# Odd heads across the partition halves by copies instead of products, with w_out's pieces first and a new list of steps

## The chip, the cores and the metric

The kernel runs on one core of one Trainium2 chip, in one launch. The metric is the device time of one execution in microseconds; the median of several runs is compared. "The profile" is one profiled execution: what each engine did and when, with the transfers (DMA).

## The reference, cut to what matters

A delta-rule attention (4 batches, 8 heads, 768 tokens, 48 features per head) is followed by a feed-forward part of three products. All is float32.

```python
k_n = k / (np.linalg.norm(k, axis=-1, keepdims=True) + 1e-06)
for t in range(S):
    kt, vt, bt = (k_n[:, :, t], v[:, :, t], beta[:, :, t, None])
    y[:, :, t] = np.einsum('bhd,bhde->bhe', q[:, :, t], state)
    v_old = np.einsum('bhde,bhd->bhe', state, kt)
    state = state + bt[:, :, :, None] * np.einsum('bhd,bhe->bhde', kt, vt - v_old)
# x: the outputs y, one row of 384 features for each of 3072 tokens
a = x @ w1                # 384 x 1024
b = x @ w2                # 384 x 1024
h = a * b @ w3            # 1024 x 1024
return h @ w_out          # 1024 x 384
```

## The kernel before, in words

**Attention.** The 768 tokens are cut into 12 chunks of 64. A chunk holds all four batches and eight heads at once: two batches lie on partitions 0 to 63, the other two on 64 to 127 (`half(z)`), and odd heads lie crossed, on the other half. The recurrence becomes, for each chunk, the inverse of a triangular 64x64 matrix for each batch and head. Two chunks share an inverse: their 32x32 diagonal blocks lie one on each partition, and VectorE eliminates them in 31 steps of two instructions (`inverse`, step names V0 to V5, lines 492 and 497 for the first two inverses, 503 and 508 for the rest). The off-diagonal 32x32 block is made with two rounds of small products (`corner`, steps e0 to e11, line 584). For the first four chunks (`TURNED`) the blocks come and go by copies, and the second round of products needs the second diagonal block of the odd heads on the other partition half: `X22`. Before the change, two products with the identity (line 598) write it into PSUM, and ScalarE copies it out (line 617).

**Norms.** `squares` (steps g0 to g5) has GpSimd square the keys of two chunks and VectorE sum them; `norms` (N0 to N5) takes the inverse norms by three Newton steps on VectorE. Both end in `across`, which moves the odd heads' numbers to the other partition half: before the change two products with the identity into a PSUM bank (line 278), then a copy of the even heads (line 283) and one out of PSUM (line 284). The banks are handed out in turn; `skip` lets one turn pass.

**Weights.** w3 and w_out are folded into one matrix of 1024 x 384, `w34` (`fold`, steps f0 to f7, line 864), since h is only used for h @ w_out. A fold takes eight matmuls, in two halves of four, and needs all of w_out and one row block of w3, transposed (`transpose_w3`, steps t0 to t15, line 855, ScalarE's copy at line 858). The weights arrive in pieces (`piece`, steps P0 to P35): P0 to P7 are w_out (128 x 384), P8 to P23 are w3 (128 x 512; P8 and P9 serve fold f0, P10 and P11 fold f1 and so on), P24 to P35 are w1 and w2. They come in 64-bit words, so each piece is a transfer on SyncE's queue into one of five `raw` buffers (line 804), two ScalarE instructions (812, 813), two on VectorE (815, 816) and an addition on GpSimd (820), which frees the buffer.

**Feed-forward.** For the first pair of chunks, `ab` multiplies x by w1 and w2 directly (line 884); the later pairs are done by `eleven` (line 1003) with sums of weights and tokens made on GpSimd, so that seven block products stand for eight. `o` multiplies by `w34` (line 1113), also with seven products, and `store` writes the result.

**Order.** Each part is a generator; a step runs it to its next `yield`. `ORDER` lists all steps by name, and every engine then works in the order in which the steps put instructions on its queue (`in_text_order`). A waiting instruction holds up all that is behind it on its engine; the transfers on SyncE's queue also go in that order. Each part has a letter of its own: k, q, v and p for loads (p in the layout for VectorE's transposes), K and Q for TensorE's transposes of the first two chunks, d for VectorE's, s for scores, u for the move of blocks to the inverse, c for the chain of states, y for the outputs, a, h, i, j for `eleven`, S and G for sums, o and x for the result.

Of the kernel before, what the change touches and what calls it, by code (L numbers as in the profile page):

```python
# [36 lines left out]


ORDER = """
V0 P0 k0 beta P18 P13 P0 P18 P0 P0 P18 P18 g0 P11 beta P13 K0 K0 P11 P10 beta P13 P13 q0 P10 g0  # L40
g0 K0 K0 K0 P11 Q0 P11 P10 P3 P3 k1 g0 g0 P12 P8 P9 P3 Q0 Q0 Q0 g0 g0 g0 g0 Q0 s0 g0 N0 P3 P10 k2
q1 P8 P8 P9 s0 P12 s0 P2 P8 s0 s0 s0 u0 K1 K1 p2 P5 K1 K1 K1 P12 g1 t3 P2 P2 P12 Q1 Q1 P2 u0 P1
P9 P9 Q1 Q1 Q1 u0 t2 s0 t2 d2 d2 P5 s1 s1 P4 s1 P5 s1 s1 s1 g1 P1 P1 g1 g1 P6 t3 u1 u1 N0 N0 t0
P5 u1 t10 V0 V0 P7 P14 V0 V0 V0 t1 P4 P4 t5 t0 P1 f1 P6 V0 V0 P4 P6 P6 V0 V0 V0 t10 t1 t5 P7 f0
P7 P7 f0 P16 V0 V0 V0 P14 P14 V0 V0 P16 P16 t4 t4 f1 f2 P19 P19 s0 f1 f2 P14 s1 f0 V0 P19 t6 V0
V0 P19 V0 P17 k3 p2 v1 t11 P17 P17 P17 P15 t6 f2 f5 t11 P16 V0 V0 g1 V0 V0 V0 V0 V1 P15 P15 P15
t9 t9 f5 f5 V0 v0 V0 t8 t8 V0 f3 t7 P20 P20 P20 f4 P22 V0 t7 f3 V0 V0 P23 P20 P21 P24 V0 P22 V0
V0 P22 V0 d2 f3 P22 f4 t14 g1 g1 g1 g1 t12 e0 e0 e0 e0 f4 g1 d2 p3 e0 s2 N1 s2 s2 P26 t14 f7 e1
P21 e1 e0 e0 P26 t12 e1 P21 P21 P24 s2 n0 e0 n0 f6 p3 d3 d3 c0 P23 e1 P30 p4 s2 s2 P23 P23 d3 u2
c0 e1 d3 e1 y0 s3 P26 P26 t13 y0 P24 n1 t15 s3 s3 P30 u2 s3 P24 s3 s3 c0 c0 t15 P30 f7 c1 t13 n1  # L50
u3 u3 u2 u3 V1 c1 P25 P31 P25 e1 P25 P31 P30 P31 P31 V1 V1 P32 V1 V1 V1 V1 V1 V1 f7 e1 f6 P27 P25
P32 c1 c1 y0 b0 f6 s1 y1 V1 b2 V1 V1 P27 y1 b3 b3 v2 P32 P28 b2 P32 V1 V1 V1 V1 b1 b0 V1 N1 N1
P29 P27 n2 P28 P28 P28 b0 b0 V1 y1 V1 V1 b1 b1 b1 c1 a03 P35 a01 P27 P29 P29 P29 V1 V1 V1 a01 a03
a02 V1 V1 V1 P33 d4 P34 V1 V1 V1 b7 V1 V2 a02 d4 a05 a05 b7 a00 k4 g2 a01 a01 a04 a04 V1 V1 V1
a06 a00 V1 V1 P33 a06 a02 a02 b3 b3 g2 a00 a00 c1 g2 g2 a07 P35 P34 e2 e2 e2 a07 b5 b5 k5 e2 b2
e2 P34 P33 p4 d4 d4 c2 v3 g2 g2 n2 c2 P33 P35 P35 g2 b4 e2 e2 n3 n3 e2 b6 c2 c2 e3 b6 b2 a03 y2
c2 b4 e3 P34 g2 g2 a04 e3 a03 p5 d5 d5 p5 y2 b4 c2 e3 e3 e3 k6 g2 s4 N2 s4 b7 b7 b4 a04 s4 s4 s4
e3 s4 b6 T u4 T T s4 e3 d5 d5 N2 b6 s5 s5 s5 s5 s5 s5 s5 s5 a06 a06 N2 T a07 a05 a07 u5 c3 c3 b5
b5 V2 g3 a05 g3 p6 v5 V2 V2 c3 c3 V2 oD0 y3 v4 g3 V2 y3 y3 V2 V2 V2 V2 oA0 V2 V2 V2 V2 d6 V2 S0
S0 S0 S0 W d6 S0 S0 S0 g3 S0 S0 c3 V2 xA0 oB0 xB0 V2 V2 V2 oA0 k7 V2 V2 S0 S0 S0 V2 S0 S0 S0 V2  # L60
oB0 xB0 V2 xA0 xA0 G1 oC0 a10 a10 a10 S0 xC0 xC0 V2 a10 V2 V2 oC0 xC0 a10 xD0 a10 V2 h10 s4 V2
i10 a12 a12 h10 h10 V2 j10 V2 V2 V2 V2 V2 h10 W W xC0 i10 g3 c3 V2 g3 V2 j12 n4 a12 i12 xD0 a12
a12 p6 d6 h10 d6 c4 g3 g3 a12 n5 n4 V2 g3 g3 i10 e4 c4 h12 e4 a11 p7 e4 W h12 h12 a11 e4 e4 i12
e5 i12 e4 N3 h12 s6 s6 s6 s6 j11 c4 c4 a11 y4 y4 a11 h12 h11 c4 d7 d7 e5 e5 p7 c4 a11 i11 c5 n5
a11 h11 c5 e5 e5 e5 h11 a13 k8 g4 d7 d7 s7 h11 s7 a13 s7 s7 s7 s7 s7 i11 i11 a13 h11 a13 u7 s6 s6
c5 c5 h13 u6 s6 a13 a13 h13 i13 i13 h13 j13 h13 h13 S1 s6 V3 V3 V3 g4 p8 V3 y5 y5 V3 V3 V3 V3 V3
i13 S1 V3 V3 v6 y5 oC1 d8 V3 oA1 S1 S1 g4 V3 V3 V3 V3 d8 n6 oD1 V3 V3 xA1 S1 oA1 v7 n7 c5 V3 V3
V3 S1 V3 xA1 oB1 xB1 g4 xA1 a20 S1 a20 V3 V3 V3 oB1 j20 xB1 xC1 k9 p8 V3 S1 xD1 V3 V3 V3 V3 G2
oC1 a20 a20 h20 xC1 xC1 a20 V3 V3 a20 h20 i20 V3 V3 V3 a22 a22 i20 V3 V3 xD1 xC1 h20 h20 h20 j22
g4 c5 g4 g4 a22 a22 d8 h22 i20 a22 V3 e6 i22 g4 d8 p9 a22 h22 h22 N3 e6 N3 i22 e6 e6 n6 h22 s7 c6  # L70
c6 a21 h22 i22 a21 a21 e6 g4 g4 N4 i21 e6 c6 s8 c6 h21 a21 s8 v8 s8 s8 n8 V4 a21 a21 h21 y6 d9 d9
s8 i21 j21 i21 y6 h21 a23 e7 s8 e7 c6 c6 s8 e7 e7 p9 i23 h21 h21 s8 e7 n7 d9 d9 a23 a23 a23 s9
k10 g5 s9 e7 s9 s9 s9 s9 a23 u8 c7 h23 s9 u9 c7 c7 a23 h23 h23 h23 V4 c7 i23 i23 S2 j23 S2 y7 h23
V4 g5 V4 V4 V4 V4 oA2 S2 S2 oD2 S2 S2 p10 V4 V4 V4 V4 V4 V4 V4 v9 V4 y7 y7 G3 c7 k11 V4 oB2 V4 V4
xA2 oA2 S2 xB2 oB2 V4 V4 V4 d10 d10 V4 V4 xB2 s9 xD2 V4 oC2 a30 a30 xC2 xC2 xD2 V4 V4 a30 V4 V4
a30 xA2 S2 oC2 xC2 p10 xA2 V4 V4 j30 h30 V4 V4 a30 c7 a30 h30 i30 i30 i30 xC2 a32 a32 V4 V4 V4 V4
h30 d10 V4 V4 j32 h30 h30 n8 e8 a32 d10 h32 a32 a32 a32 c8 c8 N4 i32 h32 i32 e8 h32 e8 h32 e8 N4
g5 g5 g5 g5 g5 a31 a31 p11 g5 a31 e8 a31 e9 g5 j31 e8 g5 N5 c8 c8 i31 h32 y8 c8 d11 a31 y8 d11
p11 h31 e9 a31 s10 c8 i32 h31 i31 i31 e9 s10 a33 a33 s10 n9 e9 h31 s10 s10 s10 s10 e9 e9 a33 a33
j33 c9 d11 d11 s11 h31 s11 s11 u10 a33 S3 V5 h31 h33 v10 n9 c9 c9 s11 s11 a33 h33 s11 u11 c9 i33  # L80
i33 i33 S3 V5 h33 h33 h33 s11 s11 y9 V5 y9 oA3 oD3 S3 S3 xA3 n10 V5 V5 V5 V5 S3 y9 V5 V5 V5 V5 V5
oB3 oC3 xB3 S3 V5 G4 V5 V5 V5 V5 oB3 xB3 oA3 S3 xD3 xC3 xC3 V5 V5 xD3 a40 a40 a40 S3 oC3 s10 n10
xA3 xA3 a40 a40 V5 V5 xC3 i40 a40 V5 V5 V5 V5 h40 h40 c9 i40 i40 V5 a42 a42 V5 V5 V5 h40 h40 a42
j40 a42 h42 h40 V5 V5 V5 V5 a42 a42 V5 i42 a41 h42 V5 V5 v11 h42 h42 i42 i42 V5 j42 a41 a41 n11
h42 i41 a41 a41 n11 h41 c9 a41 h41 j41 V5 e10 e10 e10 e10 c10 c10 i41 h41 h41 h41 a43 e10 e11 i41
N5 a43 N5 a43 a43 h43 e10 e11 e11 e11 c10 c10 j43 a43 a43 h43 c10 c10 e11 e11 i43 h43 i43 i43 h43
h43 c11 c11 y10 y10 c11 oD4 oA4 S4 xC3 S4 S4 xA4 S4 S4 c11 y11 y11 y11 oB4 oA4 xA4 oC4 S4 S4 S4
xA4 xB4 oB4 G5 xB4 xC4 a50 a50 a50 a50 oC4 a50 xC4 xC4 h50 xD4 a50 h50 i50 i50 i50 h50 h50 xD4
j50 a52 a52 a52 a52 i52 h50 a52 h52 a52 h52 i52 j52 h52 h52 h52 a51 a51 a51 a51 h51 a51 a51 i51
i52 S5 a53 a53 h51 h51 h51 j51 i51 i51 a53 h53 h51 a53 a53 j53 a53 h53 h53 i53 h53 h53 xC4 i53  # L90
i53 o5 o5 x5 o5 x5 S5 S5 S5 S5 x5 o5 o5 S5 S5 S5 o5 x5 x5 x5 x5 x5 x5 x5 o5 x5 x5 x5 x5
"""


# [1 line left out]
def kernel(  # L96
# [14 lines left out]
    P = 128  # L111
# [21 lines left out]
    def half(z):  # L133
        return slice(C * z, C * z + C)
# [17 lines left out]
    def skip(tag):  # L152
        turns[tag] = turns.get(tag, -1) + 1

    def two_banks():
        return in_turn(psW, [P, 2, 512], "w", 2, "ps_w")

    def bank(shape):
        return in_turn(psF, shape, "f", 4, "ps_f")
# [107 lines left out]

    def across(src, dst, j):

        n = src.shape[1]  # L270
        ps = bank([P, CW]) if j < 3 else two_banks()[:, 0]
        ps = ps[:, 0 : n * NR * NP].rearrange("p (c r a) -> p c r a", c=n, r=NR)
        odd, even = (
            x.rearrange("p c r (a e) -> p e (c r) a", e=2) for x in (src, dst)
        )
        psv = ps.rearrange("p c r a -> p (c r) a")
        for z in range(2):
            pe.matmul(
                psv[half(1 - z)], lhsT=ident[half(z), half(z)], rhs=odd[half(z), 1],
                start=True, stop=True,  # L280
            )
        yield
        dve.tensor_copy(out=even[:, 0], in_=odd[:, 0])
        dve.tensor_copy(out=even[:, 1], in_=psv)
        yield

    def squares(j):
# [265 lines left out]
    def corner(m):  # L553
# [38 lines left out]

        if turned:
            L = late_pad
            ps2 = two_banks()
            other22 = ps2[:, 1, N // 2 : N].rearrange("p (g t) -> p g t", t=BS)
            for z in range(2):
                pe.matmul(
                    other22[half(1 - z)], lhsT=ident[half(z), half(z)],
                    rhs=TT[half(z), :, :, BS:C].rearrange("p r (a e) t -> p e (r a) t", e=2)[:, 1],  # L600
                    start=True, stop=True,
                )
            ps = products(
                lambda n, z: (U[rows(z), C * n : C * n + C], z ^ n % 2),
                lambda n, z: T11[rows(z), BS * n : BS * n + BS],
                half, ps2,
            )
        else:
            L = T11
            ps = products(  # L610
                lambda n, z: (U[rows(z), C * n + BS : C * n + C + 1], z ^ n % 2),
                lambda n, z: T11[rows(z), BS * n : BS * n + BS],
            )
        yield
        if turned:
            X22 = in_turn(work, [P, 256], "tb", 2, "tb")[:].rearrange("p (g t) -> p g t", t=BS)
            act.copy(out=X22, in_=other22)
        for z in range(2):
            x = quarter(2 * z + turned)
            act.copy(  # L620
# [682 lines left out]
```

## Time and profile before

| | us |
|---|---|
| median of 3 runs (lowest, highest) | 558.83 (557.52, 559.52) |
| the profiled execution | 559.79 |
| its span, first to last instruction | 558.0 |
| TensorE busy | 527.2 (94%) |
| VectorE busy | 392.0 (70%) |
| GpSimd busy | 253.2 (45%) |
| ScalarE busy | 181.8 (33%) |

In the page's slices a digit is the busy share in tenths of one fortieth of the span (13.95 us). PE is TensorE's matmul, PEld its weight load, DVE is VectorE, ACT ScalarE, POOL GpSimd, SP SyncE; a "q" behind the name is the queue that issues transfers. An instruction's row gives start, duration, engine, line, operation, output and inputs with partitions x elements, and in brackets the idle time before it and what ended it. A TensorE matmul in float32 leaves two records. Matmuls overlap, so that the cost of a group is read from its start to the next group's start.

### The profile page before, as it was taken

To read this page: it belongs to the slowest core of one execution; us is meant where nothing else is said; L and a number is where in the kernel's file an instruction comes from. 1 tells how busy PE (TensorE), PEld (TensorE's weight loads), DVE (VectorE), ACT (ScalarE), POOL (GpSimd) and SP (SyncE) were. 2 spreads that over 40 slices of the span, in tenths; PEclk is the share of its full clock that TensorE was granted. 3 is DMA by queue.
4 is the path that set the end of the run, shared out by engine and by line. 5 is a ranking of instruction groups with operands and counts; after the bars stand their busy time and mean duration, and the time that the engine had idled before them with its cause. 6 is when DMAs were issued, how large, how long until landed. Compare 5 with 4: busy or idle time off the path is not lost.

```text
span 558.0 us, 20019 instructions
## 1 busy us (share of the span) xinstructions
PE 527.2 (94%) x8604; PEld 452.7 (81%) x8604; DVE 392.0 (70%) x874; ACT 181.8 (33%) x361; POOL 253.2 (45%) x270
## 2 busy tenths in 40 slices
PE   3569999999999999999999999999999999999997
PEld 2456667678888998889988889988899888998897
DVE  4989989899875998568886569976658855123422
ACT  4686558954541212332012430122220112300000
POOL 8576443643549793154631448121384022441141
PEclk9977999999999999999999999999999999999999
DMA  8976975668545635346534662453322031010001
GB/s 249 222 199 186 196 177 95 163 135 159 79 65 100 111 78 105 54 74 128 104 79 76 93 117 44 86 104 52 60 64 71 15 73 27 6 54 15 2 0 58
DMA packets 197689, 52.67 MB, mean 94 GB/s; under 512 B 185344, under 2 KB 191488, under 8 KB 197600
## 3 DMA queue, kind: packets, MB, share of 16 engines
q1 hardware_dynamic: 193408, 50.59, 44.0%
q10 hardware_dynamic: 4192, 0.79, 1.0%
q8 instruction: 68, 1.11, 0.8%
q14 instruction: 21, 0.17, 0.1%
HBM read 41.25 MB, written 8.91 MB: 90 GB/s over the span
## 4 chain that ended last, share of the span: by engine, by line
PE 85%; DMA 7%; ACT 3%; SPq 3%; issue 1%; DVE 1%; POOL 0%; ACTq 0%; DVEq 0%
PE ps_f L1003 35%; PE ps_f L1113 19%; PE ps_f L884 7%; PE ps_w L663 6%; PE ps_f L864 5%; PE ps_w L759 4%; PE ps_w L584 2%; DMA raw<-in_moe_w_dram 2%; DMA raw<-in_moe_w_out_dram 2%; SPq L251 2%; PE ps_w L391 1%; PE ps_w L397 1%; DMA X<-in_q_dram 1%; PE ps_w L1113 1%; DMA ktok<-in_k_dram 1%
## 5 line engine op out<-in xcount | busy, mean ns | idle before, releaser
L1011 DVE TENSOR_TENSOR ab<-ab,ps_f 128x512 f32<-128x512 f32 x80 | 54.3, 684 | 45.1 <-PE ps_f L1003 43.8
L1050 POOL TENSOR_TENSOR ab<-ab,late 128x512 f32<-128x512 f32 x19 | 24.2, 1276 | 121.7 <-DVE ab L1011 115.6
L1003 PE MATMUL ps_f<-xT,w1s 128*128 128x256 f32 x320 | 78.6, 382 | 0.0
L1084 POOL TENSOR_TENSOR ab<-ab 128x512 f32<-128x512 f32 (+1 forms) x56 | 61.3, 1119 | 32.9 <-PE ps_f L1113 23.2
L1003 PEld LDWEIGHTS ps_f<-xT,w1s 128*128 128x128 f32 x320 | 59.9, 190 | 8.0 <-issue 0.2
L1113 PE MATMUL ps_f<-w,ab 128*128 128x192 f32 x376 | 65.0, 327 | 0.0
L1113 PEld LDWEIGHTS ps_f<-w,ab 128*128 128x128 f32 x376 | 61.5, 190 | 0.8 <-issue 0.2
L1019 ACT COPY ab<-ps_f 128x512 f32<-128x512 f32 x20 | 11.7, 587 | 121.6 <-PE ps_f L1003 121.6
L503 DVE TENSOR_TENSOR tb<-ps_w,Ub 128x31 f32<-128x31 f32 (+15 forms) x124 | 42.0, 338 | 8.7 <-ACT ps_w L483 4.7
L1113 PE MATMUL ps_f<-room,ab 128*128 128x192 f32 x272 | 47.6, 329 | 0.0
L864 PE MATMUL ps_f<-w2s,w3T 128*128 128x384 f32 x128 | 45.4, 506 | 1.4 <-ACT w3T L858 0.8
L508 DVE TENSOR_TENSOR ps_w<-ps_w,tb 128x31 f32<-128x31 f32 (+15 forms) x124 | 43.3, 349 | 4.2
L780 ACT COPY xT<-ps_w 48x256 f32<-48x256 f32 x96 | 30.5, 366 | 47.9 <-PE ps_w L759 44.8
L1113 PEld LDWEIGHTS ps_f<-room,ab 128*128 128x128 f32 x272 | 44.3, 190 | 0.7 <-issue 0.3
L1003 PE MATMUL ps_f<-xT,room 128*128 128x256 f32 x160 | 41.1, 384 | 0.0
L293 POOL TENSOR_TENSOR sq<-ktok 128x384 f32<-128x384 f32 x24 | 21.0, 884 | 43.4 <-DMA ktok<-in_k_dram 26.3
L1003 PE MATMUL ps_f<-xT,w2s 128*128 128x256 f32 x160 | 40.0, 382 | 0.0
L864 PEld LDWEIGHTS ps_f<-w2s,w3T 128*128 128x128 f32 x128 | 24.4, 197 | 17.5 <-issue 2.5
L1003 PE MATMUL ps_f<-x_room,w2s 128*128 128x256 f32 x160 | 38.5, 384 | 0.0
L417 POOL TENSOR_TENSOR PT<-PT,smask 128x512 f32<-128x512 f32 x20 | 25.5, 1280 | 27.7 <-ACT PT L415 18.9
L820 POOL TENSOR_TENSOR w<-w,raw 128x512 uint32<-128x512 uint32 x16 | 20.7, 1296 | 30.4 <-DVE w L816 15.6
L1003 PEld LDWEIGHTS ps_f<-x_room,w2s 128*128 128x128 f32 x160 | 29.7, 190 | 4.8 <-DVE late L1011 0.7
(158 smaller groups left out, 1042.5 us busy)
## 6 DMA issues: line engine op xcount, KB each, us to landing
raw<-in_moe_w_dram SPq DMA_DIRECT2D x16, 512.0 KB, 5.4
vtok<-in_v_dram SPq DMA_DIRECT2D x24, 192.0 KB, 4.3
raw<-in_moe_w_dram SPq DMA_DIRECT2D x24, 192.0 KB, 4.4
out_dram<-osb SPq DMA_DIRECT2D x46, 96.0 KB, 1.7
ktok<-in_k_dram SPq DMA_DIRECT2D x44, 96.0 KB, 3.4
raw<-in_moe_w_out_dram SPq DMA_DIRECT2D x8, 384.0 KB, 4.5
perm<-in_k_dram SPq DMA_DIRECT2D x40, 64.0 KB, 3.0
perm<-in_q_dram SPq DMA_DIRECT2D x32, 64.0 KB, 2.6
```

Of the source, the lines that this page charges most:

```text
L417: pool.tensor_tensor(out=PT, in0=PT, in1=smask[:].unsqueeze(1).to_broadcast([P, H, C]), op=ALU.mult)
L503: dve.tensor_tensor(out=tv, in0=V[:, 0 : s + 1, s : s + 1].to_broadcast([P, s + 1, n]), in1=U[:, s, s + 1 : BS].unsqueeze(1).to_broadcast( ...
L508: dve.tensor_tensor(out=o, in0=o, in1=tv, op=ALU.subtract)
L663: pe.matmul(out(ps, r, h, z), lhsT=lhs(r, h, z), rhs=rhs(r, h, z), start=True, stop=True,)
L780: act.copy(out=xT[f, p:NP:2, b : b + NR, cc, :].rearrange("p a r t -> p r a t"), in_=pyv[f, z, b : b + NR],)
L864: pe.matmul(ps[:, 0:DM], lhsT=w3Ts[jc, kc // 4][:, kc % 4 * P : kc % 4 * P + P], rhs=wo[:, kc], start=(kc == 0), stop=(kc == KF - 1),)
L884: pe.matmul(ps[:].rearrange("p b c t -> p b (c t)"), lhsT=w[:, m, js], rhs=x[:, m, :, c0:c1].rearrange("p b c t -> p b (c t)"), start=(m = ...
L1003: pe.matmul(acc[name][:, n * i : n * i + n], lhsT=ws[b][:, P * i : P * i + P], rhs=xs[x], start=new and k == 0 and i == 0, stop=k == len(t ...
L1011: dve.tensor_tensor(out=o_, in0=x, in1=acc[name], op=ALU.add)
L1050: eng.tensor_tensor(out=Z1, in0=Z1, in1=late, op=ALU.mult)
L1084: pool.tensor_tensor(out=o_, in0=x_, in1=y_, op=op)
L1113: pe.matmul(ps[b][:, b, :], lhsT=block(u, HF * f + i, z)[:, P * b : P * b + P], rhs=ws_[w][:, i], start=first and i == 0 and (b == 0 or n ...
```

## The change

Two parts of the program are rewritten, and the list of steps is a new one. `across` copies the odd heads with two VectorE copies of half the partitions each, instead of two products and a copy from PSUM; a turn of the PSUM banks is skipped, so that the banks of other parts stay as they were. In `corner`, `X22` is filled by two GpSimd copies of half the partitions each, at the step in which the first round of products is issued, instead of two products and a ScalarE copy one step later. In the new list the first w3 piece P8 and w_out's eight pieces P0 to P7 stand ahead of the other w3 pieces; before, P0, P18, P13, P11 and P10 came first, and five of w_out's pieces came after the first seven of w3. Everything else in the list is also placed anew, with about the same steps following each other; 1470 entries become 1458, as `across` has one step fewer.

```diff
-V0 P0 k0 beta P18 P13 P0 P18 P0 P0 P18 P18 g0 P11 beta P13 K0 K0 P11 P10 beta P13 P13 q0 P10 g0
-g0 K0 K0 K0 P11 Q0 P11 P10 P3 P3 k1 g0 g0 P12 P8 P9 P3 Q0 Q0 Q0 g0 g0 g0 g0 Q0 s0 g0 N0 P3 P10 k2
-q1 P8 P8 P9 s0 P12 s0 P2 P8 s0 s0 s0 u0 K1 K1 p2 P5 K1 K1 K1 P12 g1 t3 P2 P2 P12 Q1 Q1 P2 u0 P1
-P9 P9 Q1 Q1 Q1 u0 t2 s0 t2 d2 d2 P5 s1 s1 P4 s1 P5 s1 s1 s1 g1 P1 P1 g1 g1 P6 t3 u1 u1 N0 N0 t0
-P5 u1 t10 V0 V0 P7 P14 V0 V0 V0 t1 P4 P4 t5 t0 P1 f1 P6 V0 V0 P4 P6 P6 V0 V0 V0 t10 t1 t5 P7 f0
...
+V0 P8 k0 beta P0 P1 P8 P0 P8 P0 K0 K0 P8 P2 P3 q0 Q0 P0 g0 P1 P1 P1 P2 P2 P2 K0 P3 P4 P4 P3 g0
+beta P4 g0 g0 K0 Q0 Q0 K0 Q0 k1 Q0 beta P5 P6 P6 P7 g0 P7 g0 g0 g0 g0 N0 P3 P5 P6 P6 k2 q1 K1 s0
+Q1 s0 s0 K1 K1 K1 K1 P4 Q1 Q1 P5 P5 s0 s0 P7 P7 P9 P9 Q1 Q1 s0 u0 u0 P9 P9 t0 p2 d2 s0 u0 s1 s1
+s1 s1 s1 d2 P10 P11 s1 P12 P10 u1 u1 P10 P10 t2 u1 P11 P13 P14 P15 V0 P11 P11 V0 V0 t1 V0 P12 V0
+V0 P12 V0 V0 P12 P13 P13 P13 V0 g1 V0 t1 t3 t0 f0 s1 V0 P16 P15 P14 P17 P18 t3 V0 g1 g1 k3 V0 t2
...
@@ across
-        n = src.shape[1]
-        ps = bank([P, CW]) if j < 3 else two_banks()[:, 0]
-        ps = ps[:, 0 : n * NR * NP].rearrange("p (c r a) -> p c r a", c=n, r=NR)
-        odd, even = (
-            x.rearrange("p c r (a e) -> p e (c r) a", e=2) for x in (src, dst)
-        )
-        psv = ps.rearrange("p c r a -> p (c r) a")
+        skip("f" if j < 3 else "w")
+        x, y = (x.rearrange("p c r (a e) -> p e (c r) a", e=2) for x in (src, dst))
+        dve.tensor_copy(out=y[:, 0], in_=x[:, 0])
         for z in range(2):
-            pe.matmul(
-                psv[half(1 - z)], lhsT=ident[half(z), half(z)], rhs=odd[half(z), 1],
-                start=True, stop=True,
-            )
-        yield
-        dve.tensor_copy(out=even[:, 0], in_=odd[:, 0])
-        dve.tensor_copy(out=even[:, 1], in_=psv)
+            dve.tensor_copy(out=y[half(1 - z), 1], in_=x[half(z), 1])
         yield
@@ corner
-            ps2 = two_banks()
-            other22 = ps2[:, 1, N // 2 : N].rearrange("p (g t) -> p g t", t=BS)
+            X22 = in_turn(work, [P, 256], "tb", 2, "tb")[:].rearrange("p (g t) -> p g t", t=BS)
             for z in range(2):
-                pe.matmul(
-                    other22[half(1 - z)], lhsT=ident[half(z), half(z)],
-                    rhs=TT[half(z), :, :, BS:C].rearrange("p r (a e) t -> p e (r a) t", e=2)[:, 1],
-                    start=True, stop=True,
+                pool.tensor_copy(
+                    out=X22[half(1 - z)],
+                    in_=TT[half(z), :, :, BS:C].rearrange("p r (a e) t -> p e (r a) t", e=2)[:, 1],
                 )
...
-        if turned:
-            X22 = in_turn(work, [P, 256], "tb", 2, "tb")[:].rearrange("p (g t) -> p g t", t=BS)
-            act.copy(out=X22, in_=other22)
```

## The prediction, made before the changed kernel was run

> **What bounds the kernel now.** I read the page first (shares, slices, chain), then busy time by stage, then TensorE's and VectorE's instructions in order of time up to 140 us.
>
> ```profile
> PE   3569999999999999999999999999999999999997
> PEclk9977999999999999999999999999999999999999
> PE 85%; DMA 7%; ACT 3%; SPq 3%; issue 1%; DVE 1%; POOL 0%; ACTq 0%; DVEq 0%
> ```
>
> TensorE is full from the fourth slice on and carries 85% of the chain that ends last. The stages, cut where the first fold starts, where the first corner product starts, and where the first product of `ab` (L884) starts:
>
> ```profile
> 0.00:46.07 46.07, 23.51 (x493) 20.16 (x493) 34.85 (x67) 31.05 (x52) 33.59 (x46) 0.89 0.84 207
> 46.07:82.82 36.75, 36.75 (x132) 22.52 (x132) 33.10 (x85) 20.33 (x38) 17.97 (x17) 0.95 0.87 206
> 82.82:113.37 30.55, 27.76 (x822) 20.31 (x821) 27.82 (x60) 28.35 (x49) 16.16 (x14) 1.00 0.59 122
> 113.37:140.00 26.63, 26.45 (x299) 22.33 (x300) 24.95 (x67) 11.98 (x30) 8.59 (x10) 1.00 0.78 151
> 140.00:558.00 418.00, 412.69 (x6863) 367.37 (x6861) 271.26 (x599) 90.07 (x194) 176.87 (x184) 1.00 0.35 66
> ```
>
> The first numbers are length, busy TensorE, weight loads, VectorE, ScalarE, GpSimd. TensorE lacks work for 22.6 us before 46.07, for nothing up to 82.82, for 2.8 us up to 113.37, then hardly at all (of the last 5.3 us, 3.8 lie in the tail after 535). So two things can move the time: TensorE's own work after about 46 us, and the moment at which that work can start.
>
> **TensorE work removed.** The crossing of the norms is four records (two matmuls of two passes) in each of 12 calls; the crossing of the odd heads' block is four records in each of 4 corners (steps e0 to e3).
>
> ```profile
> 82.02 0.29 PE L278 MATMUL ps_f<-ss,ident 64*64 64x16 f32 x4
> 82.24 0.66 PE L855 MATMUL ps_f<-ident,w 128*128 128x128 f32 x4
> ...
> 159.74 0.43 PE L598 MATMUL ps_w<-TT,ident 64*64 64x256 f32 x2
> 159.75 0.42 PE L584 MATMUL ps_w<-T,U 33*64 33x32 f32 x8
> 160.00 0.38 PE L598 MATMUL ps_w<-TT,ident 64*64 64x256 f32 x2
> 160.22 0.78 PE L584 MATMUL ps_w<-T,U 33*64 33x32 f32 x42
> ...
> 215.40 0.26 PE L278 MATMUL ps_w<-ss,ident 64*64 64x16 f32 x4
> 215.58 0.70 PE L1003 MATMUL ps_f<-xT,room 128*128 128x256 f32 x2
> ```
>
> From start to the next group's start a crossing of norms costs 0.18 to 0.22 us, one of blocks 0.48, in which a few other products slip along, so 0.45. After 113.37 stand 9 of the former and 2 of the latter, in a stretch without idle time: 9 x 0.2 + 2 x 0.45 = 2.7 us gone for good. The other 3 and 2 lie in the start and go into the sum there.
>
> **What takes their place.** Norms: VectorE's copy out of PSUM (L284, 0.16 to 0.17 us) becomes two copies of 64x16; the row nearest to these is L283, 0.13 to 0.57 us, mostly 0.17. That is some 0.2 us more in each of 12 calls, and VectorE no longer waits on TensorE's queue for it (in before it idles 0.32 us at 22.4, and TensorE itself idles 2.35 us at 41.24 until ScalarE frees the bank). Queued behind them are the rest of the norms and the next piece; VectorE has cover after 140 us (271 of 418 us busy), so nothing there. Blocks: ScalarE's 0.37 us (L617) goes, GpSimd gets two copies of 64x256 in each corner. Its rows are 0.234 us for 64x64 (L189) and 1.08 us for 32x512 (L557); by length a line between them gives 0.6, so 1.2 us a corner, with ends 0.5 and 2.2. They stand right behind GpSimd's own block copy, and the products that read them come only after the first corner products and two ScalarE copies of 0.59 us: hidden at 1.2 us, 0.4 us late in each corner at 2.2. I take 0. Behind them in GpSimd's queue stand a w3 piece and the next block copy.
>
> The price of GpSimd work for VectorE shows at the pieces: L816 on 128x384 takes 0.56 us at 39.34, alone, and 1.52 us at 32.73, while GpSimd's L820 runs. The Trainium skill (SBUF — State Buffer, on engine ports) says that the port pair shared by the two is an exclusive lock, held for the whole instruction. The trace agrees (0.56 against 1.52 us); by that rule the eight new GpSimd copies could hold VectorE for up to their own length, which speaks against the change. Eight copies of 0.6 us are at most 4.8 us of VectorE; four of them fall near 78 to 95 us, where VectorE has 2.7 us of idle time, and four after 140 us, where it has plenty. I take 0, with 1.5 us as the upper end.
>
> **The start, in the new list.** Before, three w3 pieces and P0 (w_out) go first and five w_out pieces are loaded at 33.8 to 39.1 us; seven w3 pieces are there when the first fold starts at 46.07 (it waits 0.83 us for a w3T copy), and TensorE never waits until 82.8. Now P8 (w3) and P0 to P7 come first. I follow VectorE's queue. Up to the norms (N0) it holds one 512-wide piece and five 384-wide ones for four and two: 0.91 us instead of 1.11 three times. q0 is issued on ScalarE's queue behind two pieces instead of three, but the sums of squares still wait for k1, issued at 10.6 as before. N0 ends near 26.0 (before 26.6). From there to the transpose of the columns (L474, 43.45 before) stood 16.9 us: five 512-wide and three 384-wide pieces among them, and 1.1 us of idle time. Now it is three 384-wide (3 x 0.91), two 512-wide (2 x 1.11), four U (0.65), two K copies (1.28), two transposes (1.31), 10.1 us, with port losses 11.8: transpose at 37.8, first step of the inverse V0 near 40.2 (44.8 before). The inverse took 31.9 us with nine pieces in it; now again nine, all 512-wide (3 x 0.2 more), and three reductions of 0.46: 33.9. So it ends 2.6 us earlier, and as one piece (1.11 us) moves from behind its end into it, with four small steps of 0.4 us ahead of the next transpose of T, corner e0 is ready at about 78.7 (82.3 before).
>
> TensorE: the first fold needs P7 added on GpSimd (near 32) and the copies of t1 and t0, which stand on ScalarE behind the pieces P12 and P13; their loads wait for raw buffers that GpSimd frees at 29 to 33, so the fold starts near 43.7. But the w3 pieces now follow each other: TensorE waits in this working some 2 us for P15 and P18 and 2 us for P19 (VectorE at 65, GpSimd 67.6, transposed at 68.2). It reaches e0 near 80.6 with 44 of 64 fold matmuls and 12 of 16 w3 transposes done; before, at 82.8, 48 and 14. A fold matmul is 0.645 us (two records at 2.58 us for 8), a transpose 0.6: 2.6 + 1.2 = 3.8 us more to do until the first product of `ab`. So that starts at 80.6 + 30.55 + 3.8 - 0.9 (two block crossings) = 114.1, or at 111.3 if the extra work fills the 2.8 us of idle time there; middle 112.7, 0.7 us earlier than before.
>
> **Sum.** -2.7 (products) - 0.7 (start) + 0.85 for waits of a new list after 113 us (ends 0 and 1.7, as much again as before has there outside the tail) = -2.55 us. The profiled execution took 559.79 us for a span of 558.0, so it would be 557.2; it lies 0.96 above the median of the runs, 558.83, and on that scale the forecast is 556.3.
>
> **Rivals.**
> **(1) w3 comes too late: slower.** VectorE is in order, and P19's conversion stands ahead of the inverse's last ten steps; P19's load is queued on SP behind nine w3 pieces, k3, eight q transfers (5.4 us before) and v1, each piece waiting for a raw buffer. In my working it lands at 62 and is wanted at 65. If it lands after 70, e0 moves by the whole delay; with 5 us late, and a fold restarted slowly (24 records took 9.73 us at 46.07 and 7.91 at 56.07, nearly 2 us), it is +7 on the start: 563.3. It decides from 2.5 us late on. For it: the load rate of 206 GB/s is already 0.87 of the queues' time. Against: before, 44 to 72 us, the same loads kept pace. The Trainium skill (TensorE: Matmul & The Clock Gate, on the clock gate) says that the array runs at half rate after an idle window of about 3.4 us; the slow records behind idle stretches agree (9.73 against 7.91 us), and by it each long wait in the folds costs about these 2 us again.
> **(2) The earlier inverse carries through.** If TensorE waits for nothing in the folds, e0 starts at 78.7 or before and `ab` about 3.5 us earlier than before: -2.7 - 3.5 + 0.85, 553.5. Against it: 3.8 us of folds left over.
> **(3) Nothing measurable.** The 2.7 us come back as waits for w1 and w2 pieces between 113 and 170 us, where VectorE is 94% busy with the second inverse: 558.8.
>
> **Numbers.** Forecast 0.40 (its own range 554.5 to 558), rival 1 0.30, rival 2 0.15, rival 3 0.15. 0.3% is 1.7 us, about what a measurement here can tell from no change. Faster by more: 0.35 of the forecast and rival 2, 0.50. Within: 0.05 of the forecast and rival 3, 0.20. Slower: 0.30. Time 556.3; 8 in 10 from 552 to 564.5, rival 2 to a little past rival 1.
>
> **What would show it.** The page: some 64 TensorE records fewer, no L278 or L598 crossings. TensorE by time: first fold near 44, first `ab` product near 112.7. Right if that start moves by less than 2 us and the time from it to the end is about 2 to 2.7 us shorter. Wrong if TensorE idles over 6 us between first fold and `ab` (rival 1, with waits on ScalarE's w3T copies or on L840's pieces), or if the stretch after the first `ab` product is not shorter (rival 3).

## The result, and the profile after

The changed kernel takes 566.1 us (median of 4 runs, 565.19 to 566.43), the kernel before 559.17 us on the same chip (4 runs, 557.52 to 560.93): a ratio of 1.0121, interval 1.0087 to 1.0155. It is slower by some 7 us where 2.5 us faster was forecast, and above the range. The profiled execution took 565.19 us for a span of 563.5, the one before 559.79 for 558.0: the two profiles differ by 5.5 us, and it is these that are compared here.

From the page of the changed kernel: the slices of TensorE and of its clock, and the shares of the chain that ended last.

```profile
PE   1559998999999999999999999999999999999997
PEclk9967998999999999999999999999999999999999
PE 71%; DVE 13%; DMA 5%; ACT 4%; issue 3%; SPq 3%; POOL 0%; DVEq 0%; POOLq 0%; ACTq 0%
```

TensorE's first slices are emptier, the clock has a dip in the seventh slice (9 before), VectorE now carries 13% of the chain (1% before), and "issue", time in which an engine waited for nothing that the profile shows, has grown from 1 to 3%. Busy time by stage, cut where the first fold, the first corner product and the first `ab` product start:

```profile
0.00:45.98 45.98, 21.80 (x476) 18.45 (x477) 33.68 (x68) 31.33 (x53) 31.67 (x45) 0.85 0.89 217
45.98:82.30 36.32, 34.57 (x121) 20.59 (x121) 34.39 (x85) 20.48 (x36) 18.82 (x20) 0.96 0.76 177
82.30:115.22 32.92, 30.63 (x826) 22.72 (x826) 27.48 (x59) 26.04 (x45) 17.53 (x16) 0.95 0.63 131
115.22:140.00 24.78, 24.64 (x290) 21.03 (x289) 23.35 (x58) 11.40 (x29) 8.91 (x9) 1.00 0.83 163
140.00:563.50 423.50, 415.68 (x6833) 368.19 (x6831) 278.30 (x618) 92.04 (x197) 179.62 (x191) 1.00 0.35 66
```

The third cut is not where the kernel before was cut. Its 113.37 us is the third pair of records of that product, not the first. Before, and then after:

```profile
111.17 0.70 PE L884 MATMUL ps_f<-xT,w1s 128*128 128x256 f32 x2
112.21 0.70 PE L884 MATMUL ps_f<-xT,w1s 128*128 128x256 f32 x2 [0.34 <-POOL w1s L820]
113.37 0.67 PE L884 MATMUL ps_f<-xT,w1s 128*128 128x256 f32 x2 [0.46 <-DMA xT<-xT]
```

```profile
115.22 1.46 PE L869 MATMUL ps_f<-xT,w1s 128*128 128x256 f32 x6
116.60 0.61 PE L744 MATMUL ps_w<-KQ,S 48*48 48x64 f32 x28
```

In after the third pair starts at 116.08 us. Cut there, the two kernels compare like with like:

```profile
0.00:116.08 116.08, 87.86 (x1424) 62.52 (x1425) 96.41 (x213) 78.70 (x134) 68.22 (x80) 0.91 0.78 180
116.08:563.50 447.42, 439.46 (x7117) 388.46 (x7115) 300.79 (x674) 102.58 (x224) 188.35 (x198) 1.00 0.38 71
```

The start is 2.7 us longer (116.08 for 113.37), and from there to the end are 447.42 us (444.63 before), 2.8 us more. TensorE's idle time up to the mark is 28.2 us (25.4 before), after it 7.96 (5.49 before). Its busy time, 527.3 us, is what it was (527.2), though 64 records are gone (8540 for 8604): something has stretched the rest.

TensorE in order of time, in the new start:

```profile
42.03 1.97 PE L840 MATMUL ps_f<-ident,w 128*128 128x128 f32 x8 [4.93 <-POOL w L805]
44.47 1.11 PE L840 MATMUL ps_f<-ident,w 128*128 128x128 f32 x4 [0.48 <-POOL w L805]
45.98 7.02 PE L849 MATMUL ps_f<-w2s,w3T 128*128 128x384 f32 x16 [0.39 <-ACT w3T L843]
...
69.52 0.66 PE L840 MATMUL ps_f<-ident,w 128*128 128x128 f32 x4 [0.88 <-POOL w L805]
70.90 2.85 PE L849 MATMUL ps_f<-w2s,w3T 128*128 128x384 f32 x8 [0.73 <-ACT w3T L843]
...
92.75 1.28 PE L574 MATMUL ps_w<-T,U 33*64 33x32 f32 x64 [1.67 <-DVE PT L411]
```

It waits 4.93 us for a w3 piece that GpSimd adds (L805; at this place it waited 2.35 us before, for a ScalarE copy), twice for w3 in the middle of the folds, where it did not wait before, and 1.67 us for VectorE ahead of the second corner. The windows around that last wait, of after:

```profile
90.00:93.50 3.50, 1.83 (x116) 1.73 (x117) 3.50 (x6) 1.90 (x4) 3.22 (x5) 1.00 0.61 105
93.50:97.00 3.50, 3.46 (x95) 2.85 (x87) 3.27 (x5) 2.80 (x4) 3.36 (x4) 0.51 0.68 153
```

In the first TensorE is busy for 1.83 of 3.50 us, VectorE for all of it; in the second the granted clock is 0.51 (before: 1.00 in both), which stretches work by 1.7 us. The Trainium skill (TensorE: Matmul & The Clock Gate, Part 1) puts the half rate behind at least one idle window of about 3.4 us. The length agrees; here a wait of 1.67 us was enough, and the measurement decides.

### The profile page after: what moved, and what is told of

It is laid out like the page before. It is cut to its first block, busy times and chain, and to the rows that moved or that the text cites. A ratio compares the mean times of both kernels' runs of the same rounds, so it can differ in the third digit from the quotient of the medians.

```text
span 563.5 us, 19916 instructions
## 1 busy us (share of the span) xinstructions
PE 527.3 (94%) x8540; PEld 451.0 (80%) x8540; DVE 397.2 (70%) x886; ACT 181.3 (32%) x357; POOL 256.6 (46%) x278
## 4 chain that ended last, share of the span: by engine, by line
PE 71%; DVE 13%; DMA 5%; ACT 4%; issue 3%; SPq 3%; POOL 0%; DVEq 0%; POOLq 0%; ACTq 0%
PE ps_f L988 34%; PE ps_f L1098 17%; PE ps_w L648 5%; PE ps_w L744 3%; PE ps_f L869 3%; PE ps_f L849 3%; PE ps_w L574 2%; SPq L251 2%; PE ps_w L381 2%; DVE tb L482 2%; DVE KQ L337 1%; DVE ps_w L487 1%; PE ps_w L387 1%; DVE tb L493 1%; DVE ps_w L498 1%
## 5 line engine op out<-in xcount | busy, mean ns | idle before, releaser
L765 ACT COPY xT<-ps_w 48x256 f32<-48x256 f32 x96 | 30.4, 365 | 43.7 <-PE ps_w L744 43.2
L988 PEld LDWEIGHTS ps_f<-xT,room 128*128 128x128 f32 x160 | 29.7, 190 | 4.8 <-DVE osb L1128 0.4
L988 PEld LDWEIGHTS ps_f<-xT,w2s 128*128 128x128 f32 x160 | 30.0, 190 | 4.1
```

The lines of the kernel that those rows point to most:

```text
L765: act.copy(out=xT[f, p:NP:2, b : b + NR, cc, :].rearrange("p a r t -> p r a t"), in_=pyv[f, z, b : b + NR],)
L988: pe.matmul(acc[name][:, n * i : n * i + n], lhsT=ws[b][:, P * i : P * i + P], rhs=xs[x], start=new and k == 0 and i == 0, stop=k == len(t ...
```

## The experiments

All times are medians with the kernel before on the same chip beside them. The runs were made on several chips, so runs from different chips are compared by their ratios to the kernel before. First the change was taken apart.

**Both crossings by copies, list of before.** Edit: the new bodies of `across` (in two steps, so that the list fits) and `corner`, `ORDER` left as it was.

> The kernel before with its own list of steps; both crossings are made by copies as in the changed kernel, and the freed step of each crossing of norms is left empty. Theory L (the new list costs the time, the copies save TensorE work): 2.7 us less than before, 555.5 to 558. Theory C (the copies cost it: they hold VectorE through the shared port or come late): 562 to 566, near the changed kernel. Theory M (both halves small, each some 3 us): 559 to 562.

Measured: 569.71 us (before 560.78), ratio 1.0162 (1.0122 to 1.0202).

**Only the norms' crossing by copies, list of before.** Edit: `across` alone.

> The kernel before with its own list; only the norms cross by VectorE copies, the odd heads' blocks still by products. Theory L: 9 products' groups of 0.2 us less in the full stretch, 1.8 us faster than before, 556.5 to 558. Theory C: slower than before if VectorE's copies are what costs (over 560.5), the same as before if GpSimd's are.

Measured: 570.54 us, ratio 1.0171 (1.0132 to 1.0211).

**Only the blocks' crossing by copies, list of before.** Edit: `corner` alone.

> The kernel before with its own list; only the odd heads' blocks cross by GpSimd copies, the norms still by products. Theory L: 0.9 us faster than before, 557.5 to 559. Theory C: slower (over 560.5) if GpSimd's copies hold VectorE in the second half of the first inverses; 8 copies of 0.42 us are 3.4 us at most.

Measured: 561.56 us, ratio 1.0016 (0.9986 to 1.0045).

**The list of after, blocks by products.** Edit: `corner` of before in the changed kernel.

> The changed kernel with its new list; the odd heads' blocks cross by products again, the norms by copies. Theory L: 0.9 to 1.8 us slower than the changed kernel, 567 to 568. Theory C: back towards the kernel before, 560 to 564.

Measured: 573.61 us, ratio 1.0224 (1.0184 to 1.0265).

So the new list does not by itself make the loss: with the norms' copies the old list is slower still (ratio 1.0171 for 1.0121, about 3 us). Taking out 24 small products costs 10 us, and putting eight products back into the changed kernel costs about 6 (1.0224 for 1.0121). Neither sign goes with the work, and the first and the fourth time lie above every range given for them. The second has the sign of theory C, which is tested below. TensorE's waits show where it goes; from the run with the norms' copies, after 113 us (total in us, times, longest):

```profile
PE ps_w L389 <- issue: 2.5, 2, 1.6
PE ps_w L751 <- issue: 1.8, 2, 1.3
PE ps_w L655 <- issue: 1.3, 1, 1.3
...
PE ps_w L576 <- issue: 1.0, 2, 0.8
```

These are holes of about a microsecond inside rows of small products. The longest, in order of time:

```profile
303.27 1.15 PE L655 MATMUL ps_w<-vtok,TT 64*64 64x48 f32 x64
...
304.81 0.28 PE L383 MATMUL ps_w<-KQ 48*64 48x128 f32 x2
306.65 0.27 PE L389 MATMUL ps_w<-KQ 48*64 48x64 f32 x2 [1.56 <-issue]
```

The transfers of the same run between 303.8 and 305.4 us, in 40 slices of 0.04 us, and by queue (packets, MB, share of 16 engines):

```profile
GB/s 0 0 0 0 0 0 0 0 0 0 410 0 0 0 0 0 0 0 0 0 0 0 0 0 0 0 0 0 0 0 0 0 0 0 0 0 0 0 0 0
q8 instruction: 1, 0.02, 3.6%
```

One packet, of instructions. It starts at 304.2 and takes 3.6% of 16 x 1.6 us, 0.92 us. TensorE has run dry at 305.09, the packet is there at 305.14, and 1.5 us later TensorE goes on. The page of before counts 68 such packets in 1.11 MB, 16,384 bytes each; 17,208 records of products and weight loads came with them, some 256 to a packet. Hence **theory F**: where these pieces end in the program, against the dense rows, sets the late stalls, and each removed product moves all later ends.

**Products made but not read.** Edit, on the kernel before:

```diff
-        dve.tensor_copy(out=even[:, 1], in_=psv)
+        for z in range(2):
+            dve.tensor_copy(out=even[half(1 - z), 1], in_=odd[half(z), 1])
```

> The kernel before, with its list and all of its products, but the 12 norm crossings take the other half by two VectorE copies between partition halves instead of from the bank; the 24 products are still made and nobody reads them. VectorE does what it did in the run of norm copies under the old list (570.54 us); TensorE issues exactly what it issued in the kernel before. Theory F (TensorE's instructions arrive by DMA in pieces of 16,384 bytes, 256 instructions; in its traces each hole of 0.7 to 2.1 us in a row of small products ends 1.28 to 1.54 us after such a piece has landed, and taking out the 24 products, 96 records, moved the pieces against the rows): the late stalls go back to those of the kernel before, and the time is 559 to 562.5, the start's later first inverse step of up to 1.85 us included. Theory C (the VectorE copies themselves cost: they are slow beside GpSimd and delay what VectorE has queued): 567 to 571. In between, 563 to 566: both have a share.

Measured: 560.95 us (before 558.88), ratio 1.0041 (1.0016 to 1.0065), against 570.54 for the same copies without the products. After 113 us TensorE waits once for over 0.2 us, 0.9 us for a transfer. VectorE's copies did not make the 10 us, so theory C falls; the missing products did.

**Spare products at the start.** Edit, on the kernel before, ahead of the transposes of beta, N = 16, 32, 48, 64 and 4:

```diff
+        for _ in range(N):
+            pe.matmul(
+                ps[0 : 2 * H, 0, 0 : 2 * H], lhsT=ident[0 : 2 * H, 0 : 2 * H],
+                rhs=ident[0 : 2 * H, 0 : 2 * H], start=True, stop=True,
+            )
```

`2 * H` is 16. A product is two records and two weight loads, four instructions, so 64 of them fill a packet. They lie in TensorE's idle time; with 48 they ran from 1.42 to 4.15 us, and the next work came at 6.29.

> The kernel before with nothing changed but 16 spare 16x16 products of the identity at the very start, at about 6 us, where TensorE waits for data; 64 more records, a quarter of a piece of instructions, so that every later piece ends a quarter earlier in the program. What they take, some 0.5 us, lies in a wait of 6 us. Theory F: the stalls of the late rows move, and the three kernels with 16, 32 and 48 spare products differ from the kernel before or from one another by 2 us or more. Theory C, and any in which what matters is the work and its order: 559 to 562 in all three, as the kernel before.

> As the run with 16, with 32 spare products: half a piece of instructions, about 1 us in the wait at the start. Theory F: a time that differs from the kernel before, or from those with 16 and 48, by 2 us or more, with holes in other rows. Theory C: 559 to 562.

> As the run with 16, with 48 spare products: three quarters of a piece, about 1.5 us in the wait at the start. It is a quarter piece away from the kernel before on the other side, and moves the pieces the way that taking out 16 products at the start would. Theory F: it differs by 2 us or more from one of the other three, and is the one of them most likely to be slower, since the copies' kernels take products out. Theory C: 559 to 562.

Measured: 567.56, 566.23 and 568.28 us (before 558.88), ratios 1.0153 (1.0112 to 1.0193), 1.0139 (1.0100 to 1.0178), 1.0155 (1.0127 to 1.0182). Seven to nine microseconds more for products that lie in idle time and that nobody reads. The longest of TensorE's waits after 113 us with 48:

```profile
PE ps_w L391 <- issue: 2.1, 2, 1.2
PE ps_w L759 <- issue: 1.6, 2, 0.9
PE ps_w L663 <- issue: 1.0, 1, 1.0
PE ps_w L584 <- issue: 0.6, 1, 0.6
```

> The kernel before with 64 spare 16x16 products of the identity at the start: 256 records, a whole piece of instructions, so that every later piece begins at the same instruction as in the kernel before. They lie at 1.4 to some 5 us; the first data came at 6.3 us in the run with 48. Theory F (where the pieces end against the dense rows sets the late stalls): the time goes back to 558 to 562, though 16, 32 and 48 gave 567.56, 566.23 and 568.28. Theory S (spare products at the start cost by themselves, for instance by what they do to the start or to the granted clock, more with more of them): 566 to 570 again. A time of 562.5 to 565.5 leaves both a part.

Measured: 561.01 us (before 559.5), ratio 1.0015 (0.9991 to 1.0040). With a whole piece more, the time is back, and so are the waits, here all of them after 113 us:

```profile
PE ps_w L759 <- DVE X L703: 0.5, 1, 0.5
PE ps_f L884 <- POOL w1s L820: 0.4, 2, 0.2
PE ps_w L759 <- issue: 0.2, 1, 0.2
```

Theory S, that spare products cost by themselves, falls. The period is a piece.

> The kernel before with 4 spare products at the start: 16 records, a sixteenth of a piece. Theory F: how far the time is from 559 tells how narrow the favourable place is: 559 to 561 if the dense rows leave some room, 563 or more if the list sits at an edge. No theory but F makes it differ from 559.5 by more than 1.5 us.

Measured: 562.36 us (before 560.35), ratio 1.0033 (1.0005 to 1.0061), between the two readings that were given. Sixteen more instructions cost 0.3 to 3.4 us.

Its profiled execution took 568.11 us, and shows something else besides two holes. VectorE and GpSimd there:

```profile
172.24 6.47 DVE L283 COPY wt<-wt 128x16 f32<-128x16 f32 x1
```

```profile
172.02 2.50 POOL L417 TENSOR_TENSOR PT<-PT,smask 128x512 f32<-128x512 f32 x2
174.47 1.96 POOL L936 TENSOR_TENSOR room<-room,w 128x384 f32<-128x384 f32 x2
176.38 1.62 POOL L293 TENSOR_TENSOR sq<-ktok 128x384 f32<-128x384 f32 x2
177.94 0.73 POOL L1084 TENSOR_TENSOR ab<-ab 128x256 f32<-128x256 f32 x1
```

The copy of the even heads, 0.17 us at this place in the kernel before, lasts from 172.24 to 178.71 us, through seven GpSimd instructions, and ends as the last of them ends (178.68); TensorE waits 3.3 us behind it. The profile with 32 spare products (572.59 us, 6 above its median) has the same copy at 6.45 us. So these two profiles are not instruction supply alone, and what such a copy adds to the medians was not tested.

The holes of half a microsecond or more marked "issue" after 113 us, counted in the profiled executions, whose own times stand beside the medians:

| kernel | median us | profiled us | holes | their sum, us |
|---|---|---|---|---|
| before | 558.83 | 559.79 | 0 | 0 |
| products kept unread, list of before | 560.95 | 559.93 | 0 | 0 |
| before with 64 spare | 561.01 | 561.99 | 0 | 0 |
| blocks by copies, list of before | 561.56 | 561.66 | 3 | 2.1 |
| before with 16, 32, 48 spare | 567.56, 566.23, 568.28 | 570.14, 572.59, 568.24 | 6, 4, 6 | 7.3, 3.8, 5.3 |
| both by copies, norms by copies, list of before | 569.71, 570.54 | 571.99, 571.46 | 5, 6 | 5.8, 6.4 |
| after | 566.1 | 565.19 | 1 | 1.1 |
| after, blocks by products | 573.61 | 573.22 | 4 | 3.8 |
| after with 16, 32, 48 spare | 574.85, 573.58, 570.15 | 576.14, 575.71, 568.73 | 4, 3, 3 | 4.3, 3.3, 2.4 |

All the runs of this case together have 50 such holes. All 50 end 1.22 to 1.62 us after a piece landed, while the pieces lie mostly 4 to 9 us apart: that stretch behind a landing is only some 5% of the time. The table counts whole holes only: windows at half the clock that follow some of them (3.4 us, so 1.7 us lost) and rows that are merely slowed are not in it. With 16 spare products the holes (7.3 us) and two such windows (3.4 us) about cover the 10.4 us by which that span is longer than that of before; with 48 the holes are 5.3 of 8.5 us.

**The changed kernel in other phases.** The same edit on it, N = 16, 32, 48.

> The kernel after with 16 spare products at the start, a quarter of a piece. Theory F: its time depends on the same thing, and one of the three phases 16, 32, 48 is likely to be off its 566.1 us by 2 us or more. If the whole difference to the kernel before is the phase, one of the four gives 557 to 561; if the list and the copies cost by themselves, the best of the four stays over 563, the later start (the first product into the block results at 115.22 instead of 113.37 us) and the two clock windows more at half speed being in it whatever the phase.

> As with 16, half a piece: after has 128 records fewer than before in all, so this brings the last pieces back to the instructions that they begin at in the kernel before, though under another list. Theory F gives no sign for it in advance: 557 to 575. If list and copies cost by themselves: 563 or more.

> As with 16, three quarters of a piece. Theory F gives no sign in advance: 557 to 575. If list and copies cost by themselves: 563 or more; if nothing but the phase were the cost, the lowest of the four phases of the kernel after would be within 2 us of the kernel before.

Measured: 574.85, 573.58 and 570.15 us (before 559.5), ratios 1.0248 (1.0201 to 1.0295), 1.0236 (1.0188 to 1.0284), 1.0168 (1.0132 to 1.0204). The changed kernel, too, stands at the best of its four phases. So the phase is why removing products in the old list cost 10 us, but not why after is slower than before: the mean ratios over four phases, 1.011 and 1.019, differ by some 4.5 us, the two best by 6.8.

**Both crossings by copies, all 32 products made and not read, list of before.**

> The kernel before, with its list, both crossings by copies as in the kernel after, and all 32 products still made and read by nobody: TensorE issues what it issued in the kernel before, so the pieces of instructions begin where they did. The same copies without the products gave 569.71 us. Theory F: 560 to 562.5; the copies alone cost at most 2. Were it 565 or more, the two kinds of copies together would cost something that neither cost alone (GpSimd copying blocks beside VectorE's copies).

Measured: 561.82 us (before 560.35), ratio 1.0028 (1.0006 to 1.0050). The copies cost about 1.6 us, 0.3 to 2.8, and bring nothing. What is left of the loss, about 5 us, lies in the new list or in its meeting with the new stream.

**The two lists joined.** First at step b0 (about 110 us). In the new start with the old rest, 10 spare products stand for the 10 missing ones and 22 are made unread, so that the rest has the pieces of before; the old start with the new rest has copies only.

> The list of after up to the first step b0 (about 110 us), from there the steps that are left in the order of the list before. Both crossings by copies; the 10 products that belong to the new start are left out and replaced by 10 spare ones at the very beginning, the other 22 are made and not read, so that after the start every piece of instructions begins where it did in the kernel before. Theory P (the difference at favourable pieces lies in the new start: in the profile of after TensorE idles 27.4 us before 113 us against 23.8, and has 3.4 us more at half the clock): 563 to 567. Theory R (it lies in the rest): 559.5 to 562.

> The list of before up to the first step b0, then the steps that are left in the order of the list after; copies, no products, as in the kernel after, so that after the start every piece begins where it does in the kernel after. Theory P: the loss of the new start goes, 559.5 to 562.5. Theory R: 564 to 567, as the kernel after. The stall of 1.1 us at 311 us that the kernel after shows should stay under both.

Measured: 571.61 us, ratio 1.0205 (1.0172 to 1.0238), and 565.58 us, ratio 1.0102 (1.0061 to 1.0144). The first tells nothing: behind its join stands a wait that neither list has, and the clock is halved for 6.8 us around its end.

```profile
PE ps_w L778 <- POOL PT L430: 5.6, 1, 5.6
```

The second lies in the range of theory R, but has two waits of 1.3 us behind the join that after does not have (for a transfer at 115 us, for VectorE at 170).

Then at about 185 us, where the two lists have done the same steps but for three, built in the same way.

> As the run of the new start with the rest of the old list, but joined later and where the two lists have done the same steps but for three, at about 185 us (before the first product of oB0); 20 products of the new part are replaced by 20 spare ones at the very beginning, the last 12 are made and not read, so that from the join on every piece of instructions begins where it did in the kernel before. In that earlier run one wait of 5.6 us right behind the join, and two clock windows at half speed after it, were the join's own; here none over 1 us is expected. The profiles put the kernel after 2.75 us behind at the first product into the second stage (198.89 against 196.14) and another 2.7 us behind from there to the start of the tail (541.22 against 535.75). Theory B (both parts of the new list cost about that): 561.5 to 563.5. Theory P (all in the part up to the join): 564 to 567. Theory R (all in the rest): 559.5 to 561.5.

> The list of before up to the same point, then the rest of the list after; copies and no products, so that from the join on every piece begins where it does in the kernel after. Theory B: 561.5 to 564. Theory P: 559.5 to 562. Theory R: 564 to 567, with the stall at about 311 us still there. Stalls of the copies under the old list before the join (1.4 us in two holes at 154 to 166 us in the run of block copies) may add up to 1.5 us under each theory.

Measured: 568.75 us (564.88 to 572.4), ratio 1.0155 (1.0107 to 1.0203), and 564.34 us, ratio 1.0087 (1.0066 to 1.0108). Busy time up to 113 us and from there on: before, after, new to 185 us, old to 185 us.

```profile
0.00:113.00 113.00, 88.02 (x1444) 62.95 (x1444) 95.41 (x210) 79.73 (x137) 67.36 (x77) 0.94 0.78 184
113.00:558.00 445.00, 439.15 (x7160) 389.74 (x7160) 296.58 (x665) 102.06 (x224) 185.83 (x194) 1.00 0.38 72
```

```profile
0.00:113.00 113.00, 84.78 (x1414) 60.47 (x1415) 93.54 (x206) 76.33 (x130) 65.81 (x79) 0.91 0.79 183
113.00:563.50 450.50, 442.54 (x7128) 390.51 (x7126) 303.66 (x681) 104.96 (x228) 190.75 (x200) 1.00 0.38 71
```

```profile
0.00:113.00 113.00, 84.61 (x1420) 60.19 (x1424) 93.16 (x204) 75.80 (x129) 66.68 (x78) 0.92 0.81 183
113.00:563.10 450.10, 443.31 (x7199) 392.13 (x7190) 305.98 (x683) 105.52 (x229) 190.93 (x200) 1.00 0.38 71
```

```profile
0.00:113.00 113.00, 85.75 (x1420) 61.54 (x1420) 99.69 (x213) 79.03 (x135) 69.78 (x81) 0.95 0.79 183
113.00:562.30 449.30, 441.51 (x7120) 390.27 (x7120) 299.86 (x674) 101.56 (x222) 186.84 (x197) 1.00 0.38 71
```

With the new list to 185 us TensorE has done as little by 113 us as in after (84.61 and 84.78 us of work, 88.02 before). Its profile has a wait of 6.0 us for GpSimd's w3 piece (4.93 in after), the waits at about 70 us, and the clock at 0.54 from 93.5 to 97. Behind 113 us it has no hole of half a microsecond and idles 6.8 us (before 5.85). That profile took 564.88 us, the shortest of its six runs, 3 us more than the copies with unread products; the median is 7 us more. With the old list to 185 us the dip at 93.5 is gone (1.00), and the later part keeps two supply holes (1.0 us at 311, as in after, and 0.65 at 240); but the old part shows a wait of 2.1 us for a transfer at 111 us here, and the run costs 2.5 us over the copies with unread products. So the start's waits go with the new list: shown. That they make some 3 of the 5 us, and the holes in the rest 1 or 2, is read from these profiles and not shown by the medians: 568.75 lies above all ranges given, 564.34 in that of theory R, and the two runs exceed the copies' run by more together (9.5 us) than after does (some 5). The parts do not add, and an exact split stays open.

## Why the prediction was wrong, step by step

**Start: forecast 0.7 us earlier, 2.7 later.** The mark was misread: 113.37 us is the third pair of records of the first `ab` product, whose first pair starts at 111.17. So 112.7 was a forecast for that third pair, and it came at 116.08. N0 ended at 25.6 us (26.0 forecast). Behind it VectorE's stretch was mis-sized: 10.1 us of work plus 1.7 for the port were put down up to the transpose of the columns, which came at 40.43, not 37.8. The five pieces in it took 8.3 us for the 6.7 so given (the last, 512 wide, 0.88 + 1.41 us where 1.11 was counted), and VectorE waited 1.7 us where no wait was counted.

The first fold started at 45.98 for 43.7. Ahead of it TensorE stood 4.93 us for a w3 piece: P10, which VectorE finished at 40.09 and GpSimd at 41.97. The prediction had followed P7 ("near 32"; GpSimd ended it at 33.65) and the copies of t1 and t0; in the new list the transposes of P10 (t2), which fold f1 needs, stand on TensorE's queue ahead of t1, which fold f0 needs. e0's products started at 82.30 for 80.6, with 44 of 64 fold matmuls and 12 of 16 transposes done, exactly as forecast; the waits inside the folds, priced at some 2 + 2 us, came to 1.75. From e0 to the mark were 33.8 us for 32.1: TensorE still idled 2.3 us there, 1.67 of them in the wait for VectorE at 92.75 that was not foreseen, and the halved clock behind it cost 1.7.

**Products: 2.7 us gone for good.** The size was about right. Behind the mark, read from each record's start to the next one's in the two traces, the crossings take 2.0 us less and the corner products between which they had slipped (`ps_w<-T,U`) 0.6 less. But the other small products take more, 2.5 us those of `ps_w<-KQ,S` (1.1 of it is the hole), 1.1 those of `ps_w<-KQ` and 0.8 those of `ps_w<-S,KQ`, and all the large products together 0.9. The step that failed is the sum: it took TensorE's instructions as if only their durations counted. In the old list the removal brought holes and half-clock windows; in the new list one whole hole of 1.11 us is left, and slower rows. Why those rows are slower was not tested.

**Waits after the first `ab`: 0.85, ends 0 and 1.7.** Idle time there rose by 2.5 us, of which the hole is 1.1, and busy time, with 2.6 us of work less, by 0.3. Products and waits together were to bring 1.85 us and cost 2.8. No term of the sum had a place for instruction supply, though the profile of before has three such waits, 0.24 us at 98.0, 0.60 at 102.6 and 0.36 at 154.8, each ending 1.38 to 1.62 us after a piece had landed.

**Copies taken at nothing: off by 1.6 us.** The single prices were fair. A GpSimd block copy took 0.39 us at the median, for 0.6; a VectorE copy of 64x16 0.17 us. Not priced was a VectorE copy that meets a GpSimd instruction: in order of time, VectorE and GpSimd in after,

```profile
21.69 0.35 DVE L274 COPY ss<-ss 64x16 f32<-64x16 f32 x2
...
77.77 1.23 DVE L274 COPY wt<-wt 64x16 f32<-64x16 f32 x2
```

```profile
77.83 1.13 POOL L547 COPY TT<-Ub 32x512 f32<-32x512 f32 x1 [0.22 <-DVE Ub L501]
79.02 0.84 POOL L587 COPY tb<-TT 64x256 f32<-64x256 f32 x2
```

Two copies take 0.35 us while GpSimd is between instructions, and 1.23 while its block copy of 1.13 us runs: they end as it ends. The lock that the prediction cites from the Trainium skill (SBUF — State Buffer, on engine ports) agrees with these rows. The copy of 6.47 us above waited through seven instructions, not one. The 1.5 us set as its upper end is close to the 1.6 that both crossings cost, but was meant for GpSimd's new copies alone, and no run shows that the lock makes up the 1.6.

**Rivals.** The first is the nearest in time (563.3) and half right in kind: TensorE did wait on w3, with the marks that it named, ScalarE's w3T copies and L840's pieces. But between first fold and `ab` it idled 4.0 us, less than the 6 that the prediction set, and the long wait came before the first fold. The second did not come: e0's products started at 82.30, not at 78.7. The third's mark was met, the stretch behind the first `ab` product was not shorter, though not for its reason: after shows no wait of over 0.2 us for w1 or w2 there. (The 94% that this rival gives VectorE up to 170 us belong to 113.37 to 140; from 113 to 170 it was 85%.)

## What to carry to other kernels

Before a few small TensorE products are taken out of a list that was ordered by measurement, or put in, run the old kernel with a quarter, a half and three quarters of a piece of spare products at its start: if the time moves by more than the spare products take, the list is fitted to where the instruction pieces end, and an edit is only to be judged against several such phases. To price a copy, keep the product that it replaces and leave its result unread; then only the copy is measured. And where "issue" waits stand inside rows of small products, look in the trace for an instruction packet that landed shortly before each of them ended.

## What the runs showed of the hardware

TensorE's instructions come by DMA during the run, 16,384 bytes at a time; a packet took 0.9 to 2.2 us, and a TensorE starved for half a microsecond or more went on 1.22 to 1.62 us after it had landed. The rows above show why dense rows can starve: 64 records of 64x48 with their weight loads (L655, 303.27 to 304.24) are 128 instructions in 0.97 us, so a piece lasts about 1.9 us there, less than packet and restart take together. Four records of 128x256 take about 0.9 us and with their weight loads use eight. That this is what makes some piece ends harmless is argued from these rates; that the ends decide is shown by the runs with 16, 32, 48 and 64 spare products. A hole of 1.25 us was followed by 3.4 us at half the clock in the run with the norms' copies, so that a stall can cost nearly 3 us; the hole of 1.56 us in the same run was not, so the length of one hole does not decide. A VectorE copy that meets a row of GpSimd instructions can wait for the whole row: 6.47 us for 0.17.
